# Trimming the first loads, masking by TensorE and reordering the first weights of an attention and MLP kernel

## The chip, the cores and the metric

The kernel runs on one core of a Trainium2 chip. The metric is the device time of one execution in microseconds; the kernel before takes 305.17 (median of three runs, 305.13 to 305.26). The profiled execution spans 303.4 from its first to its last instruction; all times of the profile count from the start of that span. Engines: PE is TensorE, DVE is VectorE, ACT is ScalarE, POOL is GpSimd, SP is SyncE.

## The reference

Attention in a sliding window of 32 keys to each side, for 8 batches, 8 heads, 576 positions and head size 64, then two matrix products with an ELU between them, on 4608 tokens of width 512 and a hidden width of 2048.

```python
def _attn_ref(q, k, v):
    B, H, S, D = q.shape
    window = 32
    scores = (1.0 / np.sqrt(D)) * np.matmul(q, k.transpose(0, 1, 3, 2))
    pos = np.arange(S)
    mask = np.abs(pos[:, None] - pos[None, :]) <= window
    scores = np.where(mask, scores, -1000000000.0)
    scores = scores - np.max(scores, axis=-1, keepdims=True)
    attn = np.exp(scores)
    attn = attn / (np.sum(attn, axis=-1, keepdims=True) + 1e-09)
    return np.matmul(attn, v).astype(np.float32)

def _moe_ref(x, w_in, w_out):
    h = x @ w_in
    g = np.where(h > 0.0, h, np.exp(np.minimum(h, 0.0)) - 1.0)
    return (g @ w_out).astype(np.float32)

# x of _moe_ref is the attention's output as (B * S, H * D)
```

## The kernel before

The attention works on pairs of query blocks: 64 queries each, 128 keys each, all heads; pair i makes 128 tokens of x. Two pairs make a tile of 256 tokens. A tile goes through eight steps of the MLP: `mm1` makes 256 hidden columns of it (8 matmuls, 4 for each 128 columns), ScalarE takes the exponential (`e_sb`), VectorE subtracts one (`m_sb`) and takes max and min (`g_sb`, in `elu`), and `mm2` multiplies by w_out (4 matmuls of 512 columns). `kk` counts these steps over the whole kernel; work of the attention is hung into them at fixed places. The scheduling is manual: each engine runs its instructions in the order in which the code records them.

A pair (cut):

```python
    def scores(i, tag="s"):
        psS = ps_tile([128, 2, 512], FP32, tag, "psS")
        ...                                     # 32 matmuls, start=True, stop=True
        st[i] = [psS, None, None, None, tag]

    def exponential(i):                         # ScalarE: pu = exp(SCALE * psS)
    def mask(i):                                # VectorE: pm = pu * masks (0 or 1)
    def pv(i):                                  # 32 matmuls pm x V_e / V_o into psS
    def normalize(i):                           # VectorE: reciprocal, x_st = psS * rc

    def x_transpose(i):
        x_st, tag = st[i][3:]
        pt = ps_tile([128, NDO, 128], BF16, tag, "psXT")
        for do in range(NDO):
            nc.tensor.transpose(
                pt[:, do, :], x_st[:, 2 * do:2 * do + 2, :], ident)
        st[i] = pt

    def x_evac(i, eng=nc.vector):               # copy to xT, the right side of mm1
        copy_on(eng, xT_of(i), st.pop(i))
```

A tag names a place in PSUM: the next tile of a tag waits until the last one has been read. V_o is V_e moved by 64 keys (`rotate_v`, VectorE). `edges(i)` sets the ones and zeros of a V_e buffer and zero columns of a key buffer on VectorE.

The front (cut; `load_cast`, `load_v` and the weights are issued by GpSimd and cast from float32 to bf16 on the way; `load_qk` by SyncE and ScalarE):

```python
    WHOLE, HALF_A, HALF_B = (0, SJ), (0, SJ // 2), (1, SJ // 2)
    for which in range(2):
        load_qk(0, which, HALF_A, (nc.sync, nc.scalar))
    ...
    edges(0)
    edges(1)
    ...                                         # masks on GpSimd
    for m in (1, 0, 2):
        load_v(0, m)
    ...
    for which in range(2):
        load_cast(0, which, HALF_B)
    load_w_in(0)                                # a quarter: 512 hidden columns
    ...                                         # rest of masks
    for m in (3, 4):
        load_v(0, m)
    load_w_in(1)
    load_w_out(0)
    load_w_out(1)

    idle(10, "y1")                              # matmuls of zeros
    front_cast(0, HALF_A, nc.vector)
    front_transpose(0, HALF_A, nc.scalar, ("h0", "h1"))
    idle(1, "u")
    front_cast(1, HALF_A, nc.vector)
    for (j0, n), tag, eng in zip(SPLIT, ("y0", "y1"), (nc.scalar, nc.vector)):
        transpose_qk(0, 1, HALF_A, j0, n, eng, tag)
    idle(2, "h0")
    for i, tag in ((0, "s"), (1, "u")):
        scores(i, tag)
        exponential(i)
    idle(4, "y0")
    rotate_v(0, 0, 2)
    for i in (0, 1):
        mask(i)
    pv(0)
    front_transpose(0, HALF_B, nc.scalar, ("h0", "h1"))
    pv(1)
    for i in (0, 1):
        normalize(i)
    x_transpose(0)
    x_evac(0, nc.scalar)
    front_transpose(1, HALF_B, nc.vector, ("y0", "y1"))
    x_transpose(1)
    x_evac(1, nc.scalar)
    idle(3, "h1")
    ...                                         # batch 1: q, k, w_in(2), w_out(2), v, w_in(3), ...
```

The first steps, their order and the MLP (cut):

```python
    at(0, "mid", scores, 2, "s")
    at(0, "mid", scores, 3, "u")
    for i in (2, 3):
        at(0, "mid", exponential, i)
    at(0, "mid", rotate_v, 0, 2, VS - 1, (0,))
    at(0, "mid", mask, 2)
    at(0, "mid", rotate_v, 0, 2, VS - 1, (1,))
    at(1, "dve", mask, 3)
    at(1, "mid", idle, 4, "y1")
    at(1, "mid", pv, 2)
    at(1, "mid", idle, 2, "y1")
    at(2, "dve", normalize, 2)
    at(2, "mid", pv, 3)
    at(2, "mid", normalize, 3)
    for i in (2, 3):
        at(3, "mid", x_transpose, i)
        at(3, "mid", x_evac, i, nc.scalar)
        at(3, "mid", lambda n: mm2(n), i - 2)

    order = [(z, n) for z in range(2) for n in range(HALF)]   # (tile, step); HALF is 4
    order += [(z, n) for n in range(HALF, STEPS) for z in range(2)]
    order += [(t, n) for t in range(2, NT) for n in range(STEPS)]

    for kk in range(NSTEP + LAG):               # LAG is 2
        if 1 <= kk < NSTEP:
            elu(kk - 1)
        run(kk, "dve")
        if kk < NSTEP:
            mm1(kk)                             # in PSUM tag h0 or h1; records e_sb, m_sb too
        run(kk, "mid")
        for n in {2: (), 3: (), 4: (), 5: (2, 3)}.get(
                kk, (kk - LAG,) if kk >= LAG else ()):
            ...
            mm2(n)
        run(kk, "end")
```

In steps 1 and 2 `m_sb` is made by ScalarE instead of VectorE.

Of the kernel before, what the change touches and what calls it, by code (L numbers as in the profile page):

```python
# [21 lines left out]
def kernel(  # L22
# [88 lines left out]

    WHOLE, HALF_A, HALF_B = (0, SJ), (0, SJ // 2), (1, SJ // 2)
    qk_f = {}

    def load_qk(b, which, part, engs=(nc.sync, nc.sync)):
        z, nj = part
        t = lpool.tile([128, 2, nj * D], FP32, tag=f"f{which}{nj}",
                       name=f"f{which}")
        qk_f[b, which, z] = t
        src = (q, k)[which][b, :, z * NC * nj:(z + 1) * NC * nj, :].rearrange(  # L120
            "(g h) (c j) d -> c g h (j d)", h=2, j=nj)
        for h in range(2):
            engs[h].dma_start(out=t[:, h, :], in_=src[:, :, h, :])

# [3 lines left out]
    def load_cast(b, which, part):  # L128
        z, nj = part
        t = cpool.tile([128, 2, nj * D], BF16, tag=f"c{which}",  # L130
                       name=f"c{which}")
        qk_c[b, which, z] = t
        src = (q, k)[which][b, :, z * NC * nj:(z + 1) * NC * nj, :].rearrange(
            "(g h) (c j) d -> c g h (j d)", h=2, j=nj)
        for h in range(2):
            nc.gpsimd.dma_start(out=t[:, h, :], in_=src[:, :, h, :])  # L136

    def load_v(b, m):
        lo = 128 * m - WIN
        p0 = max(0, -lo)  # L140
        p1 = min(128, S - lo)
        nc.gpsimd.dma_start(  # L142
            out=V_e[b % 3][p0:p1, m, :, 0:D],
            in_=v[b, :, lo + p0:lo + p1, :].rearrange("h p d -> p h d"))
# [27 lines left out]

    def load_w_in(c):
        w = D_FF // 4
        nc.gpsimd.dma_start(
            out=w_in_sb[:, :, c * w:(c + 1) * w],
            in_=moe_w_in[:, c * w:(c + 1) * w].rearrange(
                "(o p) f -> p o f", p=128))
# [11 lines left out]
    for which in range(2):  # L190
        load_qk(0, which, HALF_A, (nc.sync, nc.scalar))

# [3 lines left out]
    def edges(i):  # L196
# [9 lines left out]
    make_identity(nc, ident)  # L206

    edges(0)
    edges(1)

    masks = cpool.tile([128, 5, QB], BF16, name="masks")
    nc.gpsimd.memset(masks, 1.0)
    nc.gpsimd.affine_select(
        out=masks, in_=masks, compare_op=ALU.is_ge, fill=0.0,
        base=0, pattern=[[0, 5], [-1, QB]], channel_multiplier=1)
    nc.gpsimd.affine_select(
        out=masks, in_=masks, compare_op=ALU.is_ge, fill=0.0,
        base=2 * WIN, pattern=[[0, 5], [1, QB]], channel_multiplier=-1)  # L220
    for m in (1, 0, 2):
        load_v(0, m)
    kinds = ["FE", "EE", "EL", "LF"]
# [13 lines left out]

    def cast_qk(b, which, part, j0, n, eng):
        z, nj = part
        if (b, which, z) not in qk_b:  # L240
            qk_b[b, which, z] = lpool.tile(
                [128, nj, 2 * D], BF16, tag=f"b{which}{nj}", name="qkb")
        t = qk_b[b, which, z]
        copy_on(eng,
                t[:, j0:j0 + n, :].rearrange("p j (h d) -> p h j d", h=2),
                qk_f[b, which, z][:, :, j0 * D:(j0 + n) * D].rearrange(
                    "p h (j d) -> p h j d", d=D))
# [20 lines left out]
    def transpose_qk(b, which, part, j0, n, evac, tag="t0", later=None):  # L268
# [14 lines left out]
        def evict():  # L283
            d = keys_or_queries(b, which)
            copy_on(evac,
                    _bap(d, [d.ap[0], [S, HP], [nj, NC], [1, n]],
                         z * NC * nj + j0),
                    _bap(pt, [pt.ap[0], [1, HP], [HP, NC], [128, n]]))
# [5 lines left out]

    st = {}

    def scores(i, tag="s"):
        psS = ps_tile([128, 2, 512], FP32, tag, "psS")
        for z in range(2):
            jb = 2 * i + z  # L300
            b, qb = jb // NQB, jb % NQB
            for h in range(H):
                hp, base = h // 2, 64 * (h % 2)
                nc.tensor.matmul(  # L304
                    psS[:, h % 2, hp * 128 + z * QB:hp * 128 + (z + 1) * QB],
                    lhsT=kT[b % 2][base:base + 64, KPAD + hp * S + QB * qb - WIN:
                                   KPAD + hp * S + QB * qb - WIN + 128],
                    rhs=qT[b % 2][base:base + 64, hp, QB * qb:QB * (qb + 1)],
                    start=True, stop=True)
        st[i] = [psS, None, None, None, tag]  # L310

    def exponential(i):
# [3 lines left out]
            pu, _bap(psS, [psS.ap[0], [1, 1024]]), AX.Exp, scale=SCALE)  # L316
        st[i][1] = pu

# [61 lines left out]

    SPLIT = ((0, 5), (5, 4))

    def front_cast(which, part, eng):
        for j0, n in SPLIT:
            cast_qk(0, which, part, j0, n, eng)

    def front_transpose(which, part, evac, tags, later=None):
        for (j0, n), tag in zip(SPLIT, tags):
            transpose_qk(0, which, part, j0, n, evac, tag, later)
# [13 lines left out]
    for which in range(2):  # L403
        load_cast(0, which, HALF_B)
    load_w_in(0)
    for mi in (0, 4):
        nc.gpsimd.affine_select(
            out=masks[:, mi, :], in_=masks[:, mi, :], compare_op=ALU.is_ge,
            fill=0.0, base=-WIN, pattern=[[0, QB]], channel_multiplier=1)
    nc.gpsimd.affine_select(  # L410
        out=masks[:, 3, :], in_=masks[:, 3, :], compare_op=ALU.is_ge,
        fill=0.0, base=128 - WIN - 1, pattern=[[0, QB]],
        channel_multiplier=-1)
    for m in (3, 4):
        load_v(0, m)
    load_w_in(1)
    load_w_out(0)
    load_w_out(1)

    idle(10, "y1")  # L420
    front_cast(0, HALF_A, nc.vector)
    front_transpose(0, HALF_A, nc.scalar, ("h0", "h1"))
    idle(1, "u")
    front_cast(1, HALF_A, nc.vector)
    for (j0, n), tag, eng in zip(SPLIT, ("y0", "y1"), (nc.scalar, nc.vector)):
        transpose_qk(0, 1, HALF_A, j0, n, eng, tag)
    idle(2, "h0")
    for i, tag in ((0, "s"), (1, "u")):
        scores(i, tag)
        exponential(i)  # L430
    idle(4, "y0")
    rotate_v(0, 0, 2)
    for i in (0, 1):
        mask(i)
    pv(0)
    front_transpose(0, HALF_B, nc.scalar, ("h0", "h1"))
    pv(1)
    for i in (0, 1):
        normalize(i)
    x_transpose(0)  # L440
    x_evac(0, nc.scalar)
    front_transpose(1, HALF_B, nc.vector, ("y0", "y1"))
    x_transpose(1)
    x_evac(1, nc.scalar)
    idle(3, "h1")


# [35 lines left out]


    at(0, "mid", scores, 2, "s")
    at(0, "mid", scores, 3, "u")
    for i in (2, 3):
        at(0, "mid", exponential, i)
    at(0, "mid", rotate_v, 0, 2, VS - 1, (0,))
    at(0, "mid", mask, 2)  # L490
    at(0, "mid", rotate_v, 0, 2, VS - 1, (1,))
    at(1, "dve", mask, 3)

    at(1, "mid", idle, 4, "y1")
    at(1, "mid", pv, 2)
    at(1, "mid", idle, 2, "y1")
    at(2, "dve", normalize, 2)
    at(2, "mid", pv, 3)
    at(2, "mid", normalize, 3)
    for i in (2, 3):  # L500
        at(3, "mid", x_transpose, i)
        at(3, "mid", x_evac, i, nc.scalar)
        at(3, "mid", lambda n: mm2(n), i - 2)
    at(4, "dve", swap_pools)

    for part, kq in ((HALF_A, 7), (HALF_B, 15)):
        for which in range(2):
            if part is HALF_B:
                at(kq - 1 + which, "mid", cast_qk, 1, which, part, 0, SJ // 2,
                   (nc.scalar, nc.vector)[which])  # L510
            at(kq + which, "mid", transpose_qk, 1, which, part, 0, SJ // 2,
               nc.scalar, "s")
# [74 lines left out]

    order = [(z, n) for z in range(2) for n in range(HALF)]
    order += [(z, n) for n in range(HALF, STEPS) for z in range(2)]
# [3 lines left out]
    def mm1(kk):  # L593
# [3 lines left out]

        tags = (f"h{h}", "s") if kk == NSTEP - 1 else (f"h{h}",)
        w = FG // len(tags)
# [12 lines left out]
        for z, ps in enumerate(psH[kk]):  # L612
            e_sb = mpool.tile([128, w, TT], FP32, tag="e_sb", name="e_sb")
            nc.scalar.activation(e_sb, ps, AX.Exp)  # L614
            m_sb = mpool.tile([128, w, TT], BF16, tag="m_sb", name="m_sb")
            if kk in (1, 2):

                nc.scalar.activation(m_sb, e_sb, AX.Copy, bias=-1.0)
            else:
                nc.vector.tensor_scalar(m_sb, e_sb, -1.0, None, ALU.add)  # L620
            m_t[kk].append(m_sb)
# [3 lines left out]
    def elu(kk, z=0):  # L625
        if z == 0:
            g_t[kk] = mpool.tile([128, FG, TT], BF16, tag="g_sb", name="g_sb",
                                   bufs=5)
        ps = psH[kk][z]
# [42 lines left out]
    for kk in range(NSTEP + LAG):  # L672
        run(kk, "first")
        if 1 <= kk < NSTEP:
            elu(kk - 1)
        run(kk, "dve")
# [3 lines left out]

        for n in {2: (), 3: (), 4: (), 5: (2, 3)}.get(
                kk, (kk - LAG,) if kk >= LAG else ()):
# [39 lines left out]
```

The softmax here doesn't subtract the row's maximum and nothing guards it: scores larger than these inputs give would overflow.

## Time and profile before

| What | us |
|---|---|
| time, median of three | 305.17 |
| span of the profiled execution | 303.4 |
| TensorE busy | 291.2 (96%) |
| VectorE busy | 241.6 (80%) |
| ScalarE busy | 169.7 (56%) |
| first mm1 matmul | 15.42 |
| matmuls of zeros, start of the last one's group | 19.61 |

The page has one row for each engine, a picture of the span in 40 slices, the DMA queues, the chain of work that ended last, and groups of instructions by line. A line of the timeline reads: start, duration, engine, line of the kernel, operation, output <- input, form, how many in a row, and in brackets the idle time of the engine before it with what ended it. In a line of the table by stages, each engine has its busy time in the stage and its number of instructions; then come the granted TensorE clock, the share of time in which the DMA engines were busy, and GB/s.

### The profile page before, as it was taken

What the parts mean: (1) busy time and instruction counts of PE and PEld (TensorE: products, weight loads), DVE (VectorE), ACT (ScalarE), POOL (GpSimd) and SP (SyncE); (2) the same over time, 40 slices, a digit from 0 to 9 for tenths busy, and PEclk for the clock granted to TensorE, in tenths of its full rate; (3) what the DMA queues carried; (4) which work ended last, traced back from release to release, by engine and by line L of the source; (5) the groups of instructions that cost most, each with busy time, mean ns of one, the idle gap of its engine ahead of it and who ended that gap; (6) DMA issues with size and microseconds to landing.
All of it is one profiled execution on the core that took longest, in us unless ns stands there. A gap on an engine that the chain in (4) does not pass through costs nothing.

```text
span 303.4 us, 7587 instructions
## 1 busy us (share of the span) xinstructions
PE 291.2 (96%) x3037; PEld 197.0 (65%) x3090; DVE 241.6 (80%) x472; ACT 169.7 (56%) x255; POOL 48.6 (16%) x68
## 2 busy tenths in 40 slices
PE   6799999999999999999999999999999999999994
PEld 2466667676666666666666666666666666666662
DVE  6877588978787988888798879887988787877664
ACT  3664657778664566546654675467535353533331
POOL 8836101720004000320023002300000000000000
PEclk9999999999999999999999999999999999999999
DMA  9999999999766978999799969996811111121011
GB/s 190 180 204 205 189 277 412 299 152 222 152 205 150 285 111 237 229 304 143 159 263 319 174 163 264 324 161 157 264 35 71 35 71 35 72 37 69 2 69 70
DMA packets 92117, 52.81 MB, mean 174 GB/s; under 512 B 76594, under 2 KB 81970, under 8 KB 92082
## 3 DMA queue, kind: packets, MB, share of 16 engines
q1 hardware_dynamic: 47330, 35.61, 43.7%
q0 software_dynamic: 42880, 10.10, 41.6%
q10 hardware_dynamic: 1872, 6.62, 5.6%
q8 instruction: 24, 0.39, 0.5%
q14 instruction: 11, 0.09, 0.1%
HBM read 36.70 MB, written 15.34 MB: 172 GB/s over the span
## 4 chain that ended last, share of the span: by engine, by line
PE 89%; DMA 3%; POOL 2%; DVE 2%; issue 2%; ACT 1%; POOLq 0%; DVEq 0%; ACTq 0%
PE ps L607 41%; PE psY L644 40%; PE psS L336 4%; PE psS L304 3%; DMA w_in_sb<-in_moe_w_in_dram 3%; PE ptx L279 1%; POOL Ve L142 1%; POOL c L136 1%; PE psXT L357 1%; ACT pu L315 1%; DVE pm L324 0%; DVE g_sb L631 0%; PE ptx L274 0%; DVE Vo L153 0%; DVE x_st L348 0%
## 5 line engine op out<-in xcount | busy, mean ns | idle before, releaser
L614 ACT ACTIVATE e_sb<-ps 128x512 f32<-128x512 f32 (+1 forms) x145 | 86.4, 596 | 118.4 <-PE ps L607 110.7
L607 PE MATMUL ps<-xT,w_in_sb 128*128 128x256 bf16 x1152 | 149.3, 273 | 0.6 <-DMA w_in_sb<-in_moe_w_in_dram 0.6
L644 PE MATMUL psY<-w_out_sb,g_sb 128*128 128x512 bf16 x526 | 139.4, 379 | 3.1 <-issue 0.8
L607 PEld LDWEIGHTS <-w_in_sb 128*128 128x128 bf16 x1152 | 110.7, 98 | 39.0 <-DMA w_in_sb<-in_moe_w_in_dram 1.1
L631 DVE SCALAR_TENSOR_TENSOR g_sb<-ps,m_sb 128x512 bf16<-128x512 f32 (+1 forms) x145 | 99.5, 686 | 13.0 <-DVE m_sb L620 0.5
L620 DVE TENSOR_SCALAR m_sb<-e_sb 128x512 bf16<-128x512 f32 (+1 forms) x143 | 61.9, 433 | 37.7 <-ACT e_sb L614 35.8
L644 PEld LDWEIGHTS <-g_sb 128*128 128x128 bf16 x576 | 54.5, 98 | 38.5 <-DVE g_sb L631 0.4
L142 POOL DMA_DIRECT2D Ve<-in_v_dram x40 | 35.5, 897 | 139.0 <-PE psS L336 79.9
L315 ACT ACTIVATE pu<-psS 128x1024 bf16<-128x1024 f32 x36 | 36.5, 1020 | 1.5 <-PE psS L304 1.5
L348 DVE TENSOR_TENSOR x_st<-psS,rc 128x512 bf16<-128x512 f32 x36 | 24.9, 692 | 1.2
L324 DVE TENSOR_TENSOR pm<-pu,masks 128x1024 bf16<-128x1024 bf16 x36 | 24.6, 683 | 0.8 <-ACT pu L315 0.6
L234 ACT CAST qkb<-f 128x768 bf16<-128x768 f32 (+1 forms) x29 | 25.0, 861 | 0.0
L336 PEld LDWEIGHTS <-pm 128*64 128x64 bf16 x576 | 11.1, 110 | 9.6 <-DVE pm L324 8.1
L336 PE MATMUL psS<-Ve,pm 128*64 128x65 bf16 x320 | 13.6, 196 | 0.8 <-DVE pm L324 0.7
L236 DVE COPY y_sb<-psY 128x512 f32<-128x512 f32 (+1 forms) x19 | 12.7, 671 | 0.8 <-PE psY L644 0.8
L304 PEld LDWEIGHTS <-kT 64*128 64x128 bf16 x576 | 9.6, 95 | 4.9 <-issue 4.0
L336 PE MATMUL psS<-Vo,pm 128*64 128x65 bf16 x256 | 12.0, 196 | 0.2 <-DVE Vo L153 0.2
L304 PE MATMUL psS<-qT,kT 64*128 64x64 bf16 x576 | 11.8, 191 | 0.5 <-DVE kT L236 0.5
L234 ACT COPY y_sb<-psY 128x512 f32<-128x512 f32 (+1 forms) x18 | 10.3, 571 | 2.8 <-DVE y_sb L236 2.8
L153 DVE COPY Vo<-Ve 64x1040 bf16<-64x1040 bf16 x24 | 10.5, 438 | 1.1 <-DMA Ve<-in_v_dram 0.3
L234 ACT COPY qT<-ptx 128x1152 bf16<-128x1152 bf16 (+2 forms) x8 | 7.6, 975 | 3.5 <-PE ptx L279 2.8
L395 PE MATMUL ps_idle<-zeros 128*128 128x512 bf16 x23 | 7.8, 450 | 1.4 <-DVE zeros L194 1.3
(36 smaller groups left out, 72.2 us busy)
## 6 DMA issues: line engine op xcount, KB each, us to landing
out_dram<-y_sb SPq DMA_DIRECT2D x35, 256.0 KB, 3.9
f<-in_q_dram SPq DMA_DIRECT2D x12, 576.0 KB, 5.7
f<-in_k_dram SPq DMA_DIRECT2D x12, 576.0 KB, 8.3
in_dram<-qkb ACTq DMA_DIRECT2D x10, 576.0 KB, 4.5
Ve<-in_v_dram POOLq DMA_DIRECT2D x24, 128.0 KB, 11.6
w_in_sb<-in_moe_w_in_dram POOLq DMA_DIRECT2D x4, 512.0 KB, 9.8
w_out_sb<-in_moe_w_out_dram POOLq DMA_DIRECT2D x4, 512.0 KB, 12.6
Ve<-in_v_dram POOLq DMA_DIRECT2D x16, 96.0 KB, 10.5
```

What stands on the lines that cost most here:

```text
L142: nc.gpsimd.dma_start(out=V_e[b % 3][p0:p1, m, :, 0:D], in_=v[b, :, lo + p0:lo + p1, :].rearrange("h p d -> p h d"))
L234: nc.scalar.copy(d_, s_)
L304: nc.tensor.matmul(psS[:, h % 2, hp * 128 + z * QB:hp * 128 + (z + 1) * QB], lhsT=kT[b % 2][base:base + 64, KPAD + hp * S + QB * qb - WIN: ...
L315: nc.scalar.activation(pu, _bap(psS, [psS.ap[0], [1, 1024]]), AX.Exp, scale=SCALE)
L324: nc.vector.tensor_mul(pm, pu, _bap(mm, [mm.ap[0], [0, H], [1, 2 * QB]]))
L336: nc.tensor.matmul(psS[QB * z:QB * (z + 1), par, hp * VD:(hp + 1) * VD], lhsT=pm[:, par * HP + hp, z * QB:(z + 1) * QB], rhs=vv[:, qb // 2 ...
L348: nc.vector.tensor_mul(x_st, _bap(psS, [psS.ap[0], [VD, HP], [512, 2], [1, D]]), _bap(rc, [rc.ap[0], [2, HP], [1, 2], [0, D]]))
L607: nc.tensor.matmul(ps[:, j, :], lhsT=w_in_sb[:, do, fo * 128:(fo + 1) * 128], rhs=xT[t][:, :, do, :], start=(do == 0), stop=(do == NDO - 1))
L614: nc.scalar.activation(e_sb, ps, AX.Exp)
L620: nc.vector.tensor_scalar(m_sb, e_sb, -1.0, None, ALU.add)
L631: nc.vector.scalar_tensor_tensor(g_t[kk][:, z * w:(z + 1) * w, :], ps, 0.0, m_t[kk][z], ALU.max, ALU.min)
L644: nc.tensor.matmul(psY[t][ts], lhsT=g_t[kk][:, j, ts * 128:(ts + 1) * 128], rhs=w_out_sb[:, s * FG + j, :], start=(s == 0 and j == 0), sto ...
```

## The change

- The first part of the queries is trimmed from 288 positions to 256 (`FRONT_A`), which is what the first four pairs' halves need; the second part covers up to position 512 (`FRONT_B`), and the last 64 positions come later (`FRONT_C`).
- All values of batch 0 that the first four pairs need are issued ahead of w_in, in half pieces where half is enough; w_in's first quarter comes as two eighths.
- For pairs 0 to 3 the mask is no longer a multiplication on VectorE: a matmul of the identity with `far` (0 in the band, -30000 outside) starts the PSUM tile, and the scores add to it; the exponential then gives zeros outside the band.
- Scores and exponentials of pairs 2 and 3 are recorded ahead of mm1(0), most matmuls of zeros are dropped, and edges(1) moves behind normalize(1).
- Tiles 0 and 1 share each w_in quarter: the order of the first eight steps becomes two of tile 0, two of tile 1, and so on. Steps 2 and 3 use the PSUM tags "s" and "u". The first mm2 follow later, `g_sb` has six buffers instead of five, and `m_sb` is always VectorE's.

It is for starting the MLP earlier and with less waiting. The diff, cut to its core:

```diff
-    WHOLE, HALF_A, HALF_B = (0, SJ), (0, SJ // 2), (1, SJ // 2)
+    HJ = SJ // 2
+    WHOLE, HALF_A, HALF_B = (0, SJ), (0, HJ), (NC * HJ, HJ)
+    FRONT_A = ((0, HJ - 1), HALF_A)
+    FRONT_B = ((NC * (HJ - 1), HJ - 1), HALF_B)
+    FRONT_C = (NC * (SJ - 2), 2)
...
     edges(0)
-    edges(1)
...                                             # far by GpSimd: 0 in the band, FAR outside
+    FAR = -30000.0
+    load_v(0, 1)
+    load_v(0, 0)
+    load_v(0, 2, LOW)
...
+    def band(i, tag):
+        psS = ps_tile([128, 2, 512], FP32, tag, "psS")
+        banded[i] = psS
+        step = QB if i == 0 else 0
+        for par in range(2):
+            nc.tensor.matmul(
+                _bap(psS, [psS.ap[0], [128, HP], [QB, 2], [1, QB]], par * 512),
+                lhsT=ident,
+                rhs=_bap(far, [far.ap[0], [0, HP], [step, 2], [1, QB]],
+                         QB - step),
+                start=True, stop=False)
     def scores(i, tag="s"):
-        psS = ps_tile([128, 2, 512], FP32, tag, "psS")
+        masked = i in banded
+        psS = banded[i] if masked else ps_tile([128, 2, 512], FP32, tag,
+                                               "psS")
...
-                    start=True, stop=True)
+                    start=not masked,
+                    stop=not masked or (z == 1 and h >= H - 2))
         st[i] = [psS, None, None, None, tag]
...
-        load_cast(0, which, HALF_B)
-    load_w_in(0)
...
+        load_cast(0, which, FRONT_B[which])
+    load_v(0, 2, HIGH)
+    load_v(0, 3)
+    load_v(0, 4, LOW)
+    load_w_in(0, 0, 2)
+    load_w_in(0, 1, 2)
     load_w_in(1)
     load_w_out(0)
+    load_v(0, 4, HIGH)
+    load_cast(0, 0, FRONT_C)
     load_w_out(1)
+    make_masks()
...                                             # casts and transposes of FRONT_A
-    idle(2, "h0")
     for i, tag in ((0, "s"), (1, "u")):
-        scores(i, tag)
+        band(i, tag)
+    for i in (0, 1):
+        scores(i)
         exponential(i)
-    idle(4, "y0")
+    idle(3, "y0")
     rotate_v(0, 0, 2)
-    for i in (0, 1):
-        mask(i)
     pv(0)
...
     for i in (0, 1):
         normalize(i)
     x_transpose(0)
+    later.pop(0)()                              # second eviction of the queries, ScalarE
     x_evac(0, nc.scalar)
-    front_transpose(1, HALF_B, nc.vector, ("y0", "y1"))
+    edges(1)
+    front_transpose(1, FRONT_B[1], BOTH, ("y0", "y1"))   # ScalarE, VectorE
     x_transpose(1)
-    x_evac(1, nc.scalar)
-    idle(3, "h1")
+    x_evac(1, nc.vector)
+    band(2, "s")
+    scores(2)
+    exponential(2)
+    band(3, "u")
+    scores(3)
+    exponential(3)
+    rotate_v(0, 2, VS - 1)
...                                             # the at(0..3, ...) lines above go
     for i in (2, 3):
+        at(0, "mid", pv, i)
+        at(0, "mid", normalize, i)
+        at(1, "mid", x_transpose, i)
+        at(1, "mid", x_evac, i, BOTH[i - 2])
+    at(6, "mid", transpose_qk, 0, 0, FRONT_C, 0, 2, nc.scalar, "s")
...
-    order = [(z, n) for z in range(2) for n in range(HALF)]
+    order = [(z, n + m) for n in range(0, HALF, 2) for z in range(2)
+             for m in range(2)]
...
+                {2: ("s",), 3: ("u",)}.get(kk, (f"h{h}",)))
...
-            if kk in (1, 2):
-
-                nc.scalar.activation(m_sb, e_sb, AX.Copy, bias=-1.0)
-            else:
-                nc.vector.tensor_scalar(m_sb, e_sb, -1.0, None, ALU.add)
+            nc.vector.tensor_scalar(m_sb, e_sb, -1.0, None, ALU.add)
...
-        if 1 <= kk < NSTEP:
-            elu(kk - 1)
+        for n in {1: (), 2: (0, 1)}.get(kk, (kk - 1,) if kk < NSTEP else ()):
+            if n >= 0:
+                elu(n)
...
-        for n in {2: (), 3: (), 4: (), 5: (2, 3)}.get(
+        for n in {2: (), 3: (), 4: (), 5: (0,), 6: (1, 2), 7: (3, 4), 8: (5, 6)}.get(
```

## The prediction

> **What bounds the kernel now.** I read the page first: engine shares, then the chain of work that ended last.
>
> ```profile
> PE 291.2 (96%) x3037; PEld 197.0 (65%) x3090; DVE 241.6 (80%) x472; ACT 169.7 (56%) x255; POOL 48.6 (16%) x68
> ...
> PE 89%; DMA 3%; POOL 2%; DVE 2%; issue 2%; ACT 1%; POOLq 0%; DVEq 0%; ACTq 0%
> ```
>
> TensorE sets the end almost everywhere. What is not TensorE lies at the start, and the diff touches only the start. So I cut the span into stages, with the cuts at the first mm1 matmul (15.42), at mm1(4) (24.45) and at mm1(9) (34.59). Columns: length, then busy time of each engine.
>
> ```profile
> 0.00:15.42 15.42, 10.70 (x144) 5.60 (x147) 11.21 (x26) 8.08 (x11) 13.30 (x27) 1.00 1.25 186
> 15.42:24.45 9.03, 8.70 (x116) 5.99 (x119) 7.02 (x14) 6.44 (x10) 3.50 (x5) 1.00 1.27 204
> 24.45:34.59 10.14, 9.98 (x96) 6.75 (x96) 6.55 (x14) 4.87 (x7) 5.07 (x6) 1.00 1.55 192
> 34.59:303.40 268.81, 261.78 (x2683) 178.67 (x2729) 216.79 (x420) 150.28 (x228) 26.74 (x30) 1.00 0.86 172
> ```
>
> From mm1(9) on TensorE runs through and the two programs are the same in all that matters. So the prediction comes down to one question: when does mm1(9) start in the changed kernel? By then both kernels have issued mm1(0) to (8), mm2(0) to (6), pairs 0 to 3 and the first transposes of batch 1. The chain in order of time shows what holds the first stage:
>
> ```profile
> 2.78 2.62 POOL Ve L142 x3
> 5.41 2.34 POOL c L136 x4
> 7.75 7.63 DMA w_in_sb<-in_moe_w_in_dram
> 15.37 0.05 issue
> 15.42 1.06 PE ps L607 x8
> ```
>
> The first w_in quarter is issued eighth on GpSimd and lands at 15.37; mm1(0) starts 0.05 later. These VectorE lines of the timeline carry the rest:
>
> ```profile
> 2.97 0.09 DVE L197 MEMSET Ve<- 128x40 bf16 x1
> 3.22 0.49 DVE L198 MEMSET Ve<- 32x520 bf16 x1 [0.16 <-DVE Ve L197]
> 3.86 0.49 DVE L199 MEMSET Ve<- 32x520 bf16 x1
> 4.41 0.14 DVE L203 MEMSET kT<- 128x64 uint32 x2
> ```
>
> This is edges(1): 1.6 us in all, done before any query has landed, so it costs nothing now.
>
> [...] eight mm1 matmuls follow each other in 0.87 us. So mm1 is 0.87, mm2 (4 of N = 512) 0.86, a band 0.43. [...] packets of GpSimd's transfers follow each other without a break from about 6 to 34 us.
>
> **The change, part by part.**
>
> *Queries and keys in.* A query half is 11% smaller and its two halves are cast separately. Before, the second half landed at 0.80 + 4.1 = 4.9, the last keys at 1.53 + 5.0 = 6.5. I put them at 4.75 and 6.4. Casts of smaller pieces (0.28 to 0.31, worked out from 0.75 for 1152 and 0.50 for 512 elements), transposes and evictions as before then give the last kT part at 8.2 (before 8.67) and scores(0) at 8.24 (before 8.82). The four band matmuls (0.86) fit between 7.25 and 8.1: free.
>
> *No mask on VectorE.* Before, pv(0) began at 11.14: exponential end, mask 0.69, pv. Now pv(0) needs pu(0) (8.69 + 1.02 = 9.7) and Vo. v is issued at 2.4 instead of 2.7, and the third load is half as long, so Vo is ready at 9.4. pv(0) at 9.75, pv(1) at 10.67. normalize(1) ends at 12.1 instead of 13.6: 1.5 us won for pairs 0 and 1.
>
> *What follows on VectorE.* edges(1) now stands behind normalize(1): 12.05 to 13.7. Only then come the copy of the last key part (0.71, to 14.4) and the copy of xT(1) (about 0.65, to 14.95).
>
> *The PSUM tag.* scores(i) is now called without its tag, so st keeps "s" for every pair, and x_transpose of pairs 1 and 3 takes "s", not "u". So xT(1) waits for ScalarE's copy of xT(0) (12.5), and band(2), also in "s", waits for VectorE's copy of xT(1): 15.0. TensorE has nothing to do from 12.8 to 15.0. Then band(2) 0.43, scores(2) 0.33, band(3) 0.43, scores(3) 0.33: mm1(0), which stands behind them, starts at 16.5.
>
> *Weights.* By the packet rates before (about 1100 per us for v at 128 B, 165 for c, 200 for w at 1024 B) the queue holds v 2.1 + c 2.9 + v 1.9 us and then an eighth at 1.4 (an estimate between those rates). With 1.2 us from last packet to landing, seen on the first quarter, the first eighth lands near 14.9, the second 16.3, w_in quarter 1 at 19.0, w_out quarter 0 at 21.6, w_in quarter 2 near 30.4. So mm1(0) doesn't wait for its weights any more; it waits for VectorE.
>
> *From mm1(0) to mm1(2).* mm1(0) 16.53; pv(2) 17.40; exponential(3) (16.8 to 17.8) holds pv(3) to 17.86; mm1(1) 18.15 to 19.02. VectorE does m_sb(0), 18.4 to 18.8, ahead of both normalizes (0.84 a pair), so x_st(2) is there at 19.67, x_st(3) at 20.5. xT(2) 19.7; its copy ends at 20.7; xT(3) in the same tag waits for that and runs at 20.75; VectorE's copy ends at 21.83; mm1(2) needs both: 21.88. Between 19.02 and 21.88 TensorE does 0.44 us of work: 2.4 lost.
>
> *From mm1(2) to mm1(9).* mm1(2) to (5) and mm2(0) follow: 26.23. mm1(6) reuses h0 and needs g_sb(4). VectorE takes 0.53 + 0.61 = 1.14 a step against 0.87 of TensorE with little mm2 between; from the end of e_sb(2) at 23.53, g_sb(4) ends at 27.04: 0.85 lost. Then mm1(6) 0.87, the late queries' transposes 0.15, mm2(1), (2) 1.73, mm1(7) 0.87, transposes 0.62, mm2(3), (4) 1.73, mm1(8) 0.87, transposes 0.62, mm2(5), (6) 1.73: mm1(9) at 36.27. Its last weights (30.4) are in time at mm1(8) (33.0).
>
> *Sum.* 36.27 - 34.59 = +1.7 us. As differences: start of mm1(0) +1.1; before, 15.42 to 34.59 was 19.17 with 16.75 of useful work (mm1 7.85, mm2 6.05, scores 0.6, pv 0.57, xT 0.44, transposes 1.24), so 2.4 lost to idle matmuls and waits; after, 16.3 useful and 3.4 lost: +0.6 more. Little after 34.59 can absorb it: TensorE is 97% busy there.
>
> **The rivals.**
>
> *It works as meant.* If mm1(0) starts with its eighth (14.9) and pairs 2 and 3 fit among mm1 without waits, 0.5 comes from the start, 0.6 from scores ahead of it, 1.9 from idle matmuls and waits dropped: -2.5 to -3, or 302.5. For it: pairs 0 and 1 do get 1.5 us earlier. Against it: the order on VectorE and the shared tag are fixed by the program. And then mm1(8) would want w_in quarter 2 near 29, before it lands: more than 1 us of the gain would go back.
>
> *The clock falls.* Nearly all idle matmuls of the front are gone, and from 12.8 to 15.0 TensorE has none. If that halves the clock, the 2.9 us of matmuls that follow double in part: +1.5 to +2 more, about 308.5. [...]
>
> *Weights late.* If small packets make w_in's eighths much slower than I put them (by over 1.5 us), mm1(0) waits for them again. The same bytes pass in nearly the same order up to w_in quarter 2, so this moves the time by under 1 us.
>
> **Range and chances.** The worked sum gives 305.2 + 1.7 = 306.9. About a fifth of the weight goes to the first rival or half of it (near 303.5), a seventh to the clock (308.5), the rest to the sum with an error of 1 us: 306.5. Range 303.8 to 308.6. 2% is 6.1 us; the whole loss in the front is hardly that, so faster by 2% would need every wait of the first 35 us gone, and slower a clock loss on top of late weights: 0.01 and 0.05.
>
> **What would show it right or wrong.** Right: scores(0) near 8.2 and pv(0) near 9.75; five memsets on VectorE between 12 and 13.7; a hole on TensorE up to about 15 that ends with VectorE's copy of xT(1); mm1(0) near 16.5 although w_in landed before 15.5; a hole before mm1(2); mm1(9) near 36.3. Wrong: mm1(0) ended by the w_in transfer, or mm1(9) before 34.6; then the sum's waits aren't there. The granted clock below 1.00 between 13 and 20 would show the second rival.

## The result, and the profile after

The changed kernel takes 308.77 us (median of four executions, 307.38 to 313.23) against 305.15: 1.0101 times the time before, 95% interval 1.0058 to 1.0145. Another six executions, made beside the experiments, gave 308.78 (307.34 to 309.65) and 1.0110 (1.0084 to 1.0135). The prediction was 306.5 and a range up to 308.6: the direction and the class (within 2%) hold, the size doesn't, since 1.3 us were forecast and 3.1 to 3.6 came. The median lies 0.2 above the range; by the ratio the time is 308.2, inside it. In the profiled execution of the first set, the 313.23, the first keys landed at 9.24 instead of 5.51, and the ratio leaves it out; so the profile below is that of the second set: span 307.2, 3.8 longer than before.

The page of the kernel after, TensorE's and the next engines' shares and the chain that ended last:

```profile
PE 293.3 (95%) x3035; PEld 197.7 (64%) x3087; DVE 240.4 (78%) x474; ACT 167.9 (55%) x253; POOL 51.5 (17%) x76
...
PE 89%; DVE 5%; issue 2%; ACT 2%; DMA 1%; SPq 0%; DVEq 0%
```

VectorE had 2% of the chain and now has 5%. Three points of 307 us are 9 us; the chain's pieces on VectorE before 29 us sum to about 10, so the front is where to look. The table by stages, with the cuts at mm1(0), mm1(4) and mm1(9):

```profile
0.00:17.64 17.64, 13.27 (x177) 6.93 (x178) 10.75 (x29) 8.50 (x12) 15.99 (x33) 0.94 1.38 182
17.64:25.02 7.38, 5.82 (x76) 4.46 (x73) 4.03 (x10) 3.40 (x5) 4.29 (x8) 0.91 1.30 202
25.02:38.37 13.35, 12.27 (x108) 7.60 (x108) 9.16 (x17) 6.09 (x9) 5.10 (x7) 1.00 1.51 194
38.37:307.20 268.83, 261.93 (x2682) 178.69 (x2729) 216.44 (x419) 149.87 (x227) 26.18 (x30) 1.00 0.83 169
```

The last stage is as long as before (268.83 against 268.81), so the whole loss is in when mm1(9) starts: 38.37 against 34.59. The chain in order of time (start, duration, engine and line) shows where the first stage is held:

```profile
11.72 0.69 DVE x_st L404
12.51 0.10 DVE Ve L206
12.61 0.15 issue
12.76 0.49 DVE Ve L207
13.31 0.10 issue
13.40 0.49 DVE Ve L208
13.95 0.11 DVE kT L212
14.09 0.52 issue
14.61 0.41 DVE xT L273
15.06 0.59 PE psS L343 x2
```

These are edges(1) (L206 to L212) behind normalize(1), then the copy of xT(1), then band(2) on TensorE: the chain that the prediction drew, each piece within 0.5 us of its place. TensorE's lines of the timeline give what follows:

```profile
15.06 0.59 PE L343 MATMUL psS<-far,ident 128*128 128x512 bf16 x2 [1.99 <-DVE xT L273]
...
17.64 1.68 PE L660 MATMUL ps<-xT,w_in_sb 128*128 128x256 bf16 x8
...
22.38 0.38 PE L413 MATMUL psXT<-ident,x_st 128*128 128x128 bf16 x4 [0.67 <-ACT xT L271]
23.28 3.65 PE L660 MATMUL ps<-xT,w_in_sb 128*128 128x256 bf16 x32 [0.52 <-DVE xT L273]
...
28.77 0.49 PE L660 MATMUL ps<-xT,w_in_sb 128*128 128x256 bf16 x3 [0.98 <-DVE g_sb L680]
```

Every wait that was named is there. What was not in the sum is in the second line: the eight matmuls of mm1(0) take 1.68 us instead of 1.05. The table by stages, asked in steps of 3.41 us, tells why (after the instruction counts come clock, DMA share and GB/s):

```profile
12.15:15.56 3.41, 1.37 (x24) 0.78 (x18) 2.90 (x9) 1.14 (x2) 3.33 (x6) 1.00 1.71 159
15.56:18.97 3.41, 3.41 (x42) 2.00 (x42) 0.56 (x1) 2.05 (x2) 2.97 (x8) 0.50 1.26 207
18.97:22.39 3.42, 2.37 (x48) 1.69 (x47) 2.34 (x6) 1.78 (x3) 0.55 (x2) 1.00 1.37 197
```

From 15.56 to 18.97 TensorE runs at a granted clock of 0.50, just when the band and score matmuls and mm1(0) are due. In six of the ten executions of the changed kernel the mean clock was 0.987 to 0.993, in the other four 0.997; one such stretch alone brings 307 us to 0.994. Those four took 307.34 to 307.50, the six 308.65 or more.

### The profile page after: what moved, and what is told of

Same layout as the page of the kernel before. It is cut to its first block, busy times and chain, and to the rows that moved or that the text cites. A ratio compares the mean times of both kernels' runs of the same rounds, so it can differ in the third digit from the quotient of the medians.

```text
span 311.5 us, 7644 instructions
## 1 busy us (share of the span) xinstructions
PE 298.1 (96%) x3087; PEld 198.8 (64%) x3087; DVE 239.8 (77%) x474; ACT 167.8 (54%) x253; POOL 51.6 (17%) x76
## 4 chain that ended last, share of the span: by engine, by line
PE 90%; DVE 4%; DMA 2%; ACT 2%; issue 1%; ACTq 0%; DVEq 0%
PE ps L660 40%; PE psY L693 39%; PE psS L359 4%; PE psS L392 3%; DMA f<-in_k_dram 2%; PE ptx L319 1%; PE psS L343 1%; DVE g_sb L680 1%; DVE x_st L404 1%; PE psXT L413 1%; DVE m_sb L669 1%; ACT pu L371 1%; ACT e_sb L667 1%; PE ptx L314 0%; DVE xT L273 0%
## 5 line engine op out<-in xcount | busy, mean ns | idle before, releaser
L693 PE MATMUL psY<-w_out_sb,g_sb 128*128 128x512 bf16 x576 | 147.3, 379 | 0.0
L380 DVE TENSOR_TENSOR pm<-pu,masks 128x1024 bf16<-128x1024 bf16 x32 | 21.8, 681 | 0.5 <-ACT pu L371 0.5
L392 PEld LDWEIGHTS <-pm 128*64 128x64 bf16 x512 | 9.7, 110 | 7.4 <-DVE pm L380 6.1
L359 PE MATMUL psS<-qT,kT 64*128 64x64 bf16 x576 | 12.6, 195 | 0.0
L392 PE MATMUL psS<-Ve,pm 128*64 128x65 bf16 x288 | 11.6, 196 | 0.1
L273 DVE CAST qkb<-f 128x768 bf16<-128x768 f32 (+5 forms) x13 | 7.1, 562 | 4.6 <-DMA f<-in_k_dram 3.3
L392 PE MATMUL psS<-Vo,pm 128*64 128x65 bf16 x224 | 10.3, 196 | 0.0
L319 PE MATMUL ptx<-ident,qkb 128*128 128x128 bf16 x71 | 6.1, 239 | 3.1 <-DVE qkb L273 3.1
```

Source lines behind the costliest of these rows:

```text
L359: nc.tensor.matmul(psS[:, h % 2, hp * 128 + z * QB:hp * 128 + (z + 1) * QB], lhsT=kT[b % 2][base:base + 64, KPAD + hp * S + QB * qb - WIN: ...
L380: nc.vector.tensor_mul(pm, pu, _bap(mm, [mm.ap[0], [0, H], [1, 2 * QB]]))
L392: nc.tensor.matmul(psS[QB * z:QB * (z + 1), par, hp * VD:(hp + 1) * VD], lhsT=pm[:, par * HP + hp, z * QB:(z + 1) * QB], rhs=vv[:, qb // 2 ...
L693: nc.tensor.matmul(psY[t][ts], lhsT=g_t[kk][:, j, ts * 128:(ts + 1) * 128], rhs=w_out_sb[:, s * FG + j, :], start=(s == 0 and j == 0), sto ...
```

## The experiments

Twelve kernels ran, up to four on one chip, each beside the kernel before; ratios are to that kernel, in brackets their 95% intervals. The theory after the first profile: the serial order (tag, edges(1), xT) makes a hole on TensorE; the hole costs its length and, in most executions, the clock. The main rival: the order on VectorE between mm1(0) and mm1(6) costs the time, whatever happens in the hole.

### The changed kernel again

No edit.

> The changed kernel once more, for a trace of a typical execution. Theory A (waits on VectorE and on the PSUM tag, as predicted): span near 305.7, last key part of the front in by 6.5, mm1(0) near 16.5 ended by the chain xT(1) copy, band, scores, and mm1(9) near 36.5[...]. Rival B (the clock fell, or the first keys landed late behind the values): typical executions too have the last keys after 7 or one or more stretches of half clock between 9 and 24, and mm1(9) is late by those.

308.78; 1.0110 (1.0084 to 1.0135). The profile above is of this run. The waits are those of theory A, but rival B holds for the clock: the first keys landed in time (5.51), and a stretch at 0.50 lies between 9 and 24 (15.56 to 18.97).

### The hole filled, nothing else

```diff
     x_evac(1, nc.vector)
+    idle(8, "h1")
     band(2, "s")
```

> The changed kernel with eight matmuls of zeros between xT(1) and band(2), where TensorE waits for VectorE: nothing is computed earlier. In the trace of the changed kernel the matmuls from 15.1 to 18.9 ran at half clock. Theory A (that half clock is a part of the loss, beside the waits): band(2) still starts near 15.1, but the clock stays full, mm1(0) ends 1.5 us earlier, the spread shrinks to about 0.5 and the median falls to about 307.3 from 308.8. Rival B (the half clock has nothing to do with the hole): median and spread as before the edit, 308.8 and 2.3.

307.57 (307.51 to 308.14, five executions); 1.0080 (1.0067 to 1.0093). No execution below clock 0.997. TensorE's timeline of this kernel:

```profile
12.77 1.89 PE L454 MATMUL ps_idle<-zeros 128*128 128x512 bf16 x8
14.98 0.59 PE L343 MATMUL psS<-far,ident 128*128 128x512 bf16 x2 [0.32 <-DVE xT L273]
...
16.72 1.05 PE L661 MATMUL ps<-xT,w_in_sb 128*128 128x256 bf16 x8
...
21.86 3.65 PE L661 MATMUL ps<-xT,w_in_sb 128*128 128x256 bf16 x32 [0.52 <-DVE xT L273]
...
27.43 1.03 PE L661 MATMUL ps<-xT,w_in_sb 128*128 128x256 bf16 x8 [1.05 <-DVE g_sb L681]
```

Band(2) starts when it did (14.98 against 15.06) and still waits for VectorE; mm1(0) starts 0.92 earlier and mm1(2) 1.42 earlier. So matmuls of zeros, which compute nothing that is used, win 1.2 us by the medians and 0.9 by the ratios: the clock's share of the loss. The two ratios' intervals touch, but the trace shows the clock held (1.00 in every window from 2.50 to 26.39), and its executions (307.51 to 308.14) lie close to the four of the changed kernel that kept it (307.34 to 307.50). With the clock held the kernel is still 2.4 us slower than before (0.008 times 305.31); that is left for the order and the waits behind it.

### The two parts of the order, alone and together

The tags put back:

```diff
-    for i in (0, 1):
-        scores(i)
+    for i, tag in ((0, "s"), (1, "u")):
+        scores(i, tag)
...
-    scores(3)
+    scores(3, "u")
```

> Only the PSUM tag is put back: pairs 1 and 3 use u for scores and x_transpose. Theory A: band(2) no longer waits for VectorE's copy of xT(1), mm1(0) about 0.7 us earlier and mm1(2) 0.2 more: time lower by 0.9 than the changed kernel (306.5 for 307.4). Rival B (clock or late keys): no change beyond 0.3.

306.87 (306.30 to 309.00); 1.0065 (1.0042 to 1.0088). Band(2) comes at 13.27, scores(2) at 15.30 after 1.43 us of waiting for VectorE's copy of the last keys, mm1(0) at 16.73, mm1(2) at 21.54.

edges(1) moved behind the copies:

```diff
-    edges(1)
     front_transpose(1, FRONT_B[1], BOTH, ("y0", "y1"))
...
     rotate_v(0, 2, VS - 1)
+    edges(1)
```

> Only edges(1) moves, behind the last rotate of the front, where VectorE waits anyway. Theory A: the last key copy is 1.4 us earlier, mm1(0) near 15.2: time lower by 1.3 (306.1). Rival B: no change beyond 0.3.

306.84 (306.44 to 307.38); 1.0054 (1.0042 to 1.0066). The copy of xT(1) is at 13.31, band(2) at 13.77, scores(3) at 15.17; mm1(0) at 16.65, mm1(2) at 21.79.

Both:

> Tag put back and edges(1) moved. Theory A: mm1(0) then waits for its first eighth at about 14.9; time lower by 1.8 (305.6), about that of the kernel before. Rival B: no change beyond 0.3, or the clock's stretches move it up and down by 1.7 at a time.

306.49 (305.52 to 308.63); 1.0048 (1.0028 to 1.0068). Of TensorE's timeline:

```profile
14.41 0.41 PE L359 MATMUL psS<-qT,kT 64*128 64x64 bf16 x16
16.22 1.05 PE L660 MATMUL ps<-xT,w_in_sb 128*128 128x256 bf16 x8 [1.40 <-DMA w_in_sb<-in_moe_w_in_dram]
```

The scores of pair 3 are 2.7 us earlier than in the changed kernel, and mm1(0) only half a microsecond earlier than with the filled hole: now it waits for its weights, as expected, but they land at 16.2 and not at 14.9. Either mend breaks the hole, and the clock holds in nearly all executions (one of six with the tags and one of eight with both have a mean clock of 0.994, none of five with edges(1) moved). By the ratios, and measured against the filled hole at 1.0080, the tags then win another 0.5 us, edges(1) 0.8 and both 1.0: far less than the 2.7 us at the scores, because the next wait, for w_in, stands right behind. These single gains are rough: the interval of the tags overlaps that of the filled hole, and in the profiles mm1(9) starts at 36.42, 36.85 and 35.94, against 37.02 with the hole filled.

### m_sb out of the way

On top of both mends, the first two `m_sb` behind the copy of xT(3) on VectorE, those of steps 2 and 4 on ScalarE:

```diff
...
-            nc.vector.tensor_scalar(m_sb, e_sb, -1.0, None, ALU.add)
+            if kk in (0, 1):
+                held_m.append((m_sb, e_sb))      # recorded behind x_evac(3)
+            elif kk in (2, 4):
+                nc.scalar.activation(m_sb, e_sb, AX.Copy, bias=-1.0)
+            else:
+                nc.vector.tensor_scalar(m_sb, e_sb, -1.0, None, ALU.add)
```

> Tag and edges mended, and VectorE relieved: m_sb(0) and m_sb(1) come after both normalizes and the copy of xT(3), m_sb(2) and m_sb(4) are ScalarE's. Theory A (VectorE's order and load hold mm1(2) and mm1(6)): x_st(3) 0.9 us earlier, mm1(2) near 20.1 instead of 21.0, and the wait of 0.8 before mm1(6) goes: 1.7 us below tag and edges alone (304.8 for 306.5). Rival B (the weights hold these steps anyway): less than 0.5.

305.78 (305.46 to 307.47); 1.0030 (1.0014 to 1.0046). mm1(2) starts at 20.31 and mm1(6) at 25.18:

```profile
20.31 3.67 PE L668 MATMUL ps<-xT,w_in_sb 128*128 128x256 bf16 x32 [0.52 <-DVE xT L273]
...
25.18 1.03 PE L668 MATMUL ps<-xT,w_in_sb 128*128 128x256 bf16 x8 [0.34 <-DVE g_sb L693]
```

Against both mends alone that is 0.7 and 1.16 earlier, with a wait for g_sb of 0.34 instead of 0.80. mm1(9) is at 34.77, 0.2 behind the kernel before and 1.2 earlier than with both mends alone (35.94). Both waits shrank as theory A had it, but the time fell by only 0.5 us by the ratios, not 1.7, and the two intervals overlap. A part of the missing gain stands at the very end: from the end of the last matmul to the end of the span it takes 4.28 us, against 3.81 to 3.90 in the profiles of the second set, the kernel before and the six other edits without this one; in the four kernels below that keep the m_sb edit it takes 4.33 to 4.39. Why is open.

### w_in ahead of the values

On top of both mends, w_in's first eighth issued ahead of the second part of the values:

```diff
         load_cast(0, which, FRONT_B[which])
+    load_w_in(0, 0, 2)
     load_v(0, 2, HIGH)
     load_v(0, 3)
     load_v(0, 4, LOW)
-    load_w_in(0, 0, 2)
     load_w_in(0, 1, 2)
```

> Tag and edges mended, and the first eighth of w_in issued ahead of the values of pairs 2 and 3. Theory A (with the waits mended the first eighth's landing at 16.2 holds mm1(0)): it lands near 14.6, mm1(0) follows scores(3) at 14.8, the values land 1.4 later, and mm1(2) is 1.1 earlier: 305.4 for 306.5. Rival B (the values then hold pv(2) as long): no change beyond 0.3.

308.29 (307.51 to 309.18); 1.0098 (1.0083 to 1.0114): worse by half a per cent than both mends alone. mm1(0) starts at 15.11, as meant, but VectorE's copies of the values now wait for landings:

```profile
15.64 0.42 DVE L161 COPY Vo<-Ve 64x1040 bf16<-64x1040 bf16 x1 [1.59 <-DMA Ve<-in_v_dram]
16.53 0.71 DVE L161 COPY Vo<-Ve 64x1040 bf16<-64x1040 bf16 x1 [0.47 <-DMA Ve<-in_v_dram]
```

x_st(2) and x_st(3) follow at 19.50 and 20.34, so mm1(2) is at 22.00, a microsecond later than without this edit; between mm1(0) and mm1(2) TensorE is thinly used (1.31 us of 3.41 from 18.43 to 21.84), and from 21.84 to 25.26 the clock is 0.50. Three of the six executions have a mean clock below 0.995; the three that kept it (307.51 to 308.45) are slower than both mends alone too. So of the two orders tried, the change's own, values ahead of w_in, is the better one.

With the m_sb edit and mm2(5) moved from step 8 to step 7 as well:

> All mends together (tag, edges, m_sb, first eighth early), and mm2(5) ahead of mm1(8), which needs the third quarter of w_in. Theory A: their gains add up except where w_in quarter 2 (landing near 31) ends the wait of mm1(8): 304.0, below the kernel before. Rival B (the first 31 us are bound by the order of the weights): not below 305.0.

307.68 (306.91 to 308.42); 1.0077 (1.0063 to 1.0092). mm1(0) at 14.84, mm1(2) at 21.64: the same price. What theory A expected failed in both runs, at the same place.

### The last hole, and pairs 2 and 3 ahead of mm1(0)

Three kernels on top of the m_sb edit. First five matmuls of zeros where TensorE waits for w_in:

```diff
     scores(3, "u")
+    idle(5, "y0")
```

> The best version so far (tags, edges(1), m_sb mended; 305.78, with mm1(0) at 16.00 after a hole of 1.3 us) with five matmuls of zeros behind scores(3), in that hole. If a thinly used TensorE there still lets the clock fall in some executions: all executions at the clock 1.00 and the median at the lower edge of the spread seen before, 305.4, spread under 0.7. Rival, that the remaining loss is the wait for w_in's first eighth and nothing of the clock: 305.8 with the same spread as before.

306.37 (305.56 to 306.79), 1.0027 (1.0014 to 1.0039): the same ratio as without them, so the rival holds for the median. No execution of eleven fell below a mean clock of 0.997, against two of ten at 0.991 and 0.993 without them, and the spread is 1.2 us instead of 2.0; so few executions don't settle whether the zeros did that. The wait for w_in is not shortened by them. In the profiled execution w_in landed at 16.5.

Then pv(2) and pv(3) with their normalizes in that hole:

```diff
     rotate_v(0, 2, VS - 1)
+    pv(2)
+    idle(3, "y1")
+    normalize(2)
+    pv(3)
+    normalize(3)
     edges(1)
...
-        at(0, "mid", pv, i)
-        at(0, "mid", normalize, i)
-        at(1, "mid", x_transpose, i)
-        at(1, "mid", x_evac, i, BOTH[i - 2])
+        at(0, "mid", x_transpose, i)
+        at(0, "mid", x_evac, i, BOTH[i - 2])
```

(idle(3, "y0") stands behind scores(3) in place of the five.)

> As the run before, but pv(2) and pv(3) with their normalizes stand ahead of mm1(0), in the hole in which TensorE waits for w_in, and ahead of edges(1) on VectorE; xT(2) and xT(3) follow mm1(0). Theory, that VectorE's order holds mm1(2): pv(2) near 15.0, pv(3) near 15.9, mm1(0) 16.5 at most, mm1(2) at 18.6 instead of 20.31 without a wait. Then the weights become the bound: w_out's first quarter (22.5) is wanted at 22.1, w_in quarter 2 (31.3) at mm1(8) near 30, so that of 1.7 us about 0.5 is left at mm1(9): 34.3, and 305.2. Rival, that VectorE's sum of work between 15 and 30 holds the g_sb chain whatever its order: mm1(6) waits longer, mm1(9) stays at 34.8, 305.5 to 305.8.

306.38 (305.76 to 309.86), 1.0051 (1.0024 to 1.0078): both expectations failed. mm1(0) is at 17.70 and not at 16.5, mm1(2) at 20.88 and not at 18.6, mm1(9) at 35.38. VectorE's timeline:

```profile
18.93 0.09 DVE L206 MEMSET Ve<- 128x40 bf16 x1
19.18 0.49 DVE L207 MEMSET Ve<- 32x520 bf16 x1 [0.16 <-DVE Ve L206]
19.82 0.49 DVE L208 MEMSET Ve<- 32x520 bf16 x1
20.37 0.11 DVE L212 MEMSET kT<- 128x64 uint32 x1
20.42 0.40 DVE L273 COPY xT<-psXT 128x512 bf16<-128x512 bf16 x1
```

It is edges(1) again, now ahead of the copy of xT(3): I moved a wait from one xT to the other. So, with edges(1) where the kernel before has it, directly behind edges(0):

> The run with pv(2) and pv(3) ahead of mm1(0), with edges(1) where the kernel before has it, directly behind edges(0). There VectorE waits 1.1 us for the first queries (2.95 to 4.03), so that 0.5 us of the 1.6 delay the first cast; the waits for landings between the casts (0.25 and 0.26) take that up again. Theory, that edges(1) on VectorE, wherever it stands between 12 and 20 us, is what held the copy of xT(3) in that run (20.42): the copy now comes with its transposes near 19, mm1(2) at 19.5 at most instead of 20.88, mm1(9) 0.5 to 1.3 earlier than 35.4, time 305.2 to 305.7. Rival, that the weights bound it anyway (w_in quarter 1 for mm1(4), w_out's first quarter, w_in quarter 2 for mm1(8)): mm1(2) early, but mm1(9) at 35 or later and 306.0 to 306.5.

306.33 (305.38 to 307.99), 1.0037 (1.0019 to 1.0055). Of TensorE's timeline and of the chain in order of time:

```profile
18.83 4.69 PE L672 MATMUL ps<-xT,w_in_sb 128*128 128x256 bf16 x40
...
31.80 1.05 PE L672 MATMUL ps<-xT,w_in_sb 128*128 128x256 bf16 x8 [0.65 <-DMA w_in_sb<-in_moe_w_in_dram]
```

```profile
12.39 10.89 DMA w_out_sb<-in_moe_w_out_dram
23.28 0.28 issue
23.56 0.52 POOL c L144
24.08 7.67 DMA w_in_sb<-in_moe_w_in_dram
31.75 0.05 issue
31.80 1.05 PE ps L672 x8
```

mm1(1) to mm1(5) now run without a break from 18.83, mm1(2) among them at 19.71. But mm1(8) waits for w_in quarter 2, whose issue stands behind a wait for w_out on GpSimd (24.08) and which lands at 31.75; in the kernel before it was issued at 18.08 and landed at 30.21. The rival is right: once VectorE is out of the way the weights set mm1(8), and mm1(9) is at 35.14. Later another 0.8 us goes (262.0 from mm1(9) to the last mm1, against 261.2 before), of which the trace shows 0.4 as a wait for a transfer of V_o. An earlier issue of w_in quarter 2 was not tried.

### The kernel before without its matmuls of zeros

```diff
-    idle(2, "h0")
...
-    idle(4, "y0")
...
-    idle(3, "h1")
...
-    at(1, "mid", idle, 4, "y1")
     at(1, "mid", pv, 2)
-    at(1, "mid", idle, 2, "y1")
```

> The kernel before with 15 of its matmuls of zeros left out (the groups of 2, 4 and 3 ahead of mm1(0), and of 4 and 2 beside pv(2)); they compute nothing that is used. If thin stretches on TensorE let the clock fall whatever the kernel: a stretch at 0.50 between 10 and 20 us in some executions, median 305.5 to 307 with a spread of over 1 us. Rival, that only the hole of the changed kernel is long enough: the clock stays 1.00 and the time is 304.5 to 305.3, since some of the groups stand in TensorE's way.

306.49 (304.92 to 307.32, 22 executions); 1.0025 (1.0013 to 1.0038), 0.8 us. 21 of the 22 have a mean clock of 0.994 or less, against 3 of the 39 executions of the unedited kernel beside them (0.992 to 0.994). The table by stages in steps of 3.41 us, this kernel:

```profile
9.59:13.01 3.42, 1.26 (x51) 1.15 (x52) 2.63 (x6) 2.29 (x4) 3.42 (x5) 1.00 1.19 193
13.01:16.42 3.41, 2.73 (x29) 1.98 (x30) 2.18 (x4) 1.80 (x4) 1.44 (x4) 0.50 1.75 184
16.42:19.83 3.41, 3.41 (x45) 2.36 (x44) 1.29 (x3) 1.99 (x3) 1.79 (x3) 0.50 1.26 202
19.83:23.25 3.42, 2.55 (x45) 1.79 (x44) 3.32 (x7) 2.11 (x4) 1.07 (x2) 1.00 1.24 206
```

So the effect doesn't belong to the changed kernel alone: with the matmuls that look like waste the old one kept the clock in 36 of 39 executions, without 15 of them in one of 22, and the change took most of them away. The rival is refuted.

## Why the prediction was right or wrong

**Queries, keys and values in.** scores(0) predicted at 8.24, measured 8.48; pv(0) 9.75, measured 10.01; normalize(1) ended at 12.41 (predicted 12.1). Right to 0.3. The casts that it worked from were misread: before, a cast of 640 elements took 0.57 to 0.79 and one of 512 0.42 to 0.57, not 0.75 for 1152; the queries' pieces of 256 measured 0.29 all the same. The mask on TensorE is nearly free, as said: the four band matmuls of pairs 0 and 1 run from 7.58 to 8.44, beside VectorE's copy of the last keys (7.61 to 8.33).

**edges(1), copies, tag.** Right: five memsets from 12.51 to 14.09 (12.05 to 13.7), band(2) at 15.06 (15.0), after a wait of 1.99. That band(2) at 15.0 agrees so well is partly luck: everything before it was 0.3 late, and the copy of xT(1) took 0.40 where I had estimated 0.65.

**mm1(0) and mm1(2).** With the clock held: mm1(0) at 16.72 against 16.53, mm1(2) at 21.86 against 21.88. The sum of the waits was right; in the unheld execution they are at 17.64 and 23.28.

**Weights.** Estimated 14.9, 16.3, 19.0, 21.6 and 30.4; landed 15.7, 17.0, 19.5, 22.1 and 30.8. All late, by 0.4 to 0.8. In the changed kernel that costs nothing, since mm1(0) waits for VectorE as predicted; but in the mended versions it is the wait that comes next, and the runs with w_in ahead showed that mm1(0) near 14.9, as the first rival had it, was bought by delaying the values.

**mm1(2) to mm1(9).** Under-sized: 14.39 predicted, 15.16 measured with the clock held (21.86 to 37.02). Half of it, 0.4, is VectorE's step, which I put at 1.14 us; in the unheld run the starts of g_sb at 25.53, 26.90, 28.03 and 29.32 are 1.13 to 1.37 apart. The other 0.4 lies behind mm1(6): there three mm1 are followed by transposes, and each then takes 0.96 to 0.97 up to the first transpose instead of 0.87, which makes 0.3; the late queries' transposes took 0.23 instead of 0.15. The kernel before shows the same 0.97 (mm1(7) at 29.66, the transposes behind it at 30.63), and the prediction passed over it.

**The clock: the step that failed.** The second rival said that the hole from 12.8 to 15.0 might halve the clock and put the time at 308.5. I gave it a seventh of the weight, an estimate of mine: in the profile of the kernel before the clock is 1.00 from start to end, so nothing measured spoke to it. The hole was there as drawn, and the clock fell in most executions. What it cost was sized well: +1.5 to +2 predicted, 1.35 at mm1(9) (38.37 against 37.02) measured, 1.2 in the medians of all executions, and 1.8 between the mean of the four executions of the second set in which it fell (309.22) and of the two in which it held (307.42). The weight was wrong: the sum of waits alone gave 306.9 with an error of 1, and it was this rival that carried the range to 308.6. I looked at the length of the gap alone, and not at the work around it. In the profile the 3.41 us with the hole (12.15 to 15.56) hold 1.37 us of work, and the next 3.41 us are at 0.50. With the matmuls of zeros added they hold 3.08 (12.74 to 16.15), and the clock stays at 1.00; in the kernel before with its matmuls of zeros removed 1.26 us (9.59 to 13.01) are followed by 0.50.

In sum, for the profile: predicted +1.7, under-sized stretch behind mm1(2) +0.75, clock +1.35: 3.8.

**What else held.** The first rival (as meant) fell, for the reasons given against it, and it stays out of reach when these are mended: the best versions, 1.0030 and 1.0027, are still slower than before, 0.4 to 0.5 us of it behind the last matmul (4.28 and 4.33 us to the end of the span, 3.85 before). The third (weights late) fell for the changed kernel and became the bound of the mended ones. No version here beats the kernel before.

## What to carry to other kernels

Before dropping matmuls that only keep TensorE busy, ask what share of each few microseconds remains filled without them, not how long the longest gap is: here, at full clock, 1.26 to 1.37 us of work in 3.41 were followed by a clock of 0.50, and 1.54 to 1.98 by 1.00. A piece of housekeeping on VectorE costs nothing only where no copy that TensorE waits for stands behind it: moved from before the first landing into the front, edges(1) held up a copy twice, at two different places (xT(1), copied at 14.61, and xT(3), at 20.42). When one wait is taken away, look up when the next one would end, here w_in's landing at 16.2, half a microsecond before the start that mm1(0) had already, before counting the gain.

## What the runs showed of the hardware

The trace's clock record gives the length of each stretch at one clock. Apart from the last one, which ends with the record, it is 300.373 us at 1.00 in the kernel before, and 3.413 at 1.00, 3.413 at 0.50, 6.827 at 1.00, 3.413 at 0.50 and 286.720 at 1.00 in the first set's profile of the changed kernel: 88, 1, 1, 2, 1 and 84 times 3.413. The records begin 3.98 and 6.27 us after the start. In eleven more profiles the tables by stages up to 24 to 28 us were asked in steps of 3.41 us, each from a start of its own; every step shows 1.00 or 0.50 and nothing between. TensorE's busy time in such a window, and the clock of the next window:

| kernel | window, us | busy us of 3.41 | clock in it | clock in the next |
|---|---|---|---|---|
| before, no matmuls of zeros | 9.59 to 13.01 | 1.26 | 1.00 | 0.50 |
| w_in ahead of the values | 18.43 to 21.84 | 1.31 | 1.00 | 0.50 |
| after | 12.15 to 15.56 | 1.37 | 1.00 | 0.50 |
| before, no matmuls of zeros, at its end | 299.73 to 303.14 | 1.54 | 1.00 | 1.00 |
| edges(1) moved | 13.01 to 16.42 | 1.88 | 1.00 | 1.00 |
| hole filled | 19.57 to 22.98 | 1.90 | 1.00 | 1.00 |
| tags put back | 12.14 to 15.55 | 1.98 | 1.00 | 1.00 |
| before, no matmuls of zeros | 13.01 to 16.42 | 2.73 | 0.50 | 0.50 |
| w_in ahead of the values | 21.84 to 25.26 | 3.26 | 0.50 | 1.00 |
| after | 15.56 to 18.97 | 3.41 | 0.50 | 1.00 |

In the seven rows at full clock, 1.26 to 1.37 us of work in the window (37% to 40%) were followed by 0.50, and 1.54 to 1.98 (45% to 58%) by 1.00. The trace of the first set, with the late keys, agrees: behind the same hole the window from 16.51 to 19.92 holds 1.31 us, and the next one is at 0.50. The longest gap inside a window doesn't sort the rows: it is 1.30 us in the second row, which fell, and 1.43 with the tags put back and 1.87 in the fourth row, which both held. The eighth row, which stays at half clock with 2.73 us, all except 0.5 of it transposes, is one case and open. These are the windows of six kernels; that the same figures hold elsewhere was not shown. Nor was it shown why four of ten executions of the changed kernel kept the clock: the two that were traced both have the stretch at 0.50. The kernel before without its matmuls of zeros, which fell in 21 of 22, is thin for longer: two windows in a row, from 6.18 to 13.01, hold 2.07 and 1.26 us, where the changed kernel has 2.99 and 1.37 from 8.73 to 15.56.
